# First pair loaded by heads, key penalties in two halves, a rest on GpSimd, twelve units reordered

## The chip, the cores and the metric

One core of one Trainium2 chip runs the whole program in one launch. The metric is the device time of one execution in microseconds (us). A profiled execution has its own time, and a span, from the first to the last instruction that the profile shows. A difference of under about 0.5% (3.5 us) is what a measurement of this kernel cannot tell from no change.

## What is computed

The reference is clustered attention followed by two MLPs. Shapes: batch 2, 8 heads, 768 tokens, head size 64, 16 clusters.

```
c_n = centroids / norm;  q_assign = argmax(q_n . c_n);  k_assign = argmax(k_n . c_n)
mask = q_assign[..., :, None] == k_assign[..., None, :]
scores = where(mask, q k^T / 8, -1e9);  attn = softmax(scores);  x = attn v
h = max(x w1, x w2, x w3);  x = h w_out            # 1536 x 512 -> 768 -> 512
h = x w_in;  g = max(0.01 h, h);  out = g w_out2   # 512 -> 2048 -> 512
```

## The kernel before, in words

Two heads make a pair, and there are 8 pairs. A pair has 6 units: one head (j) and 256 queries (g) each. A unit holds two score blocks i of 128 queries by 768 keys. Products are as precise as float32: an operand is split into a rounded part and a rest, and both go through fp32r matmuls. The cluster mask is inside the scores: 16 more contraction rows hold the one-hot cluster of a query (tile q2, rows 64 to 79) and, for a key, 0 or -2^100 (tile k2, the same rows). These are the key penalties.

The program is written in short operations whose order is fixed by hand. The string `BEGIN` gives the order of the first twelve units and of everything for pairs 1 to 3 that runs beside them; `ORDER` gives the repeating order after that, and it is not touched. An operation goes to one engine, and each engine runs its own in the order in which the string has them, waiting where an operand is not there. So an operation that waits holds everything behind it on that engine. The DMAs of all steps are issued by SyncE (SP), in the same order, one after the other.

Names in the string: `S i:n` scores of block i of unit n (PE, L659; `SA` and `SB` are its two halves, unit 0 alone), `M` the row maximum (DVE, L665), `X` the exponentials (ACT, L671), `R` the inverse of the row sums (DVE, L679, L680), `Q` the normalisation (POOL, L685), `T k:n` transposes (PE, L692), `E` their way out of PSUM (ACT L705 or DVE L707), `V` the product with the values (PE, L716), `Y` its store. For pair p: `LD@p` loads q and k, `QH KH QL KL` round them and take the rests (L419 to L430), `Dq Dk Dl Dm Da Db` copy them to the operand tiles by DMA (L598), `G C H Na Nb W FA FB O P` find the clusters and make the one-hot rows.

Pair 0 has a way of its own, since nothing can hide it. `Z`, a head (a, b) and a letter make its operands without DMAs: q and r round the queries into q1 and q2, k and j the keys into the two halves of k1 (ACT, L419), l and m are the rests of queries (L427) and keys (L430). `Gq` and `Gk` are the products of queries and keys with the centroids (PE, L465), both heads in one; `Na Nb W FA FB` with q or k find the clusters (DVE, L476 to L516); `UQ` and `UK` turn the one-hot of head a (PE, L532), `CQ` and `CK` copy it into q2 and k2 (ACT), `OT`, `PA` and `D2` do the same for head b through a DMA. `Hd` is a one-column copy on POOL which waits for the key one-hot and so holds POOL back until then. `I n` is n idle matmuls on zeros (`nought`): PE work whose result nobody reads, as the two runs of `WARM` are. Unit 0 and 1 are head a, units 2 and 3 head b.

Of the kernel before, what the change touches and what calls it, by code (L numbers as in the profile page):

```python
# [10 lines left out]
BF16 = mybir.dt.bfloat16  # L11
AF = mybir.ActivationFunctionType
ALU = mybir.AluOpType
# [4 lines left out]
P = 128  # L18
B, H, S, D = 2, 8, 768, 64
C = 16  # L20
# [3 lines left out]
G = 256  # L24
# [22 lines left out]
)  # L47

BEGIN = (
    "Zaq Zbr Gq Zar Zal Naq Zbj Gk Nbq Wq FAq FBq Zaj Nak Nbk Zbq I3 UQ Wk Zak FAk CQ I1 G@1 SA0:0 FBk UK  "  # L50
# [14 lines left out]
)  # L65
AFTER = 12

# [8 lines left out]
ENGINE = {  # L76
    "QH": "A", "QH@1": "P", "QH@2": "P", "QL": "D", "QL@1": "P", "KH": "P", "KL": "P", "W": "P"
}
WARM = (7, 2)
PACE = 0.16  # L80
HALF = S // 2
WP = 512
# [6 lines left out]
def clustered_attention_mlps(  # L89
# [16 lines left out]
    nc = tc.nc  # L106
# [120 lines left out]
    def open_hidden():  # L227

        m["w1"] = mlp.enter_context(tc.tile_pool(name="w1", bufs=1))
# [89 lines left out]
    with ExitStack() as att:  # L319
# [25 lines left out]
        gain, base, gain2, base2 = (lines[:, i : i + 1] for i in range(4))  # L345
# [3 lines left out]
        def several(pool, shape, names, dtype=F32):  # L349
            return [pool.tile(shape, dtype, name=x) for x in names]  # L350

        raw_in = [several(raws, [P, S], (f"rq{i}", f"rk{i}")) for i in range(2)]
# [7 lines left out]
        opnd = [  # L360
            [
                tuple(
                    opn.tile([D + C if x[1] == "2" else P, S], F32R, name=f"{x}_{i}_{j}")
                    for x in ("q1", "q2", "k1", "k2")
                )
                for j in range(2)
            ]
            for i in range(2)
# [32 lines left out]
        st = {}  # L401

        def load_pair(p, what):
            s = st.setdefault(p, {})
            for x in what:
                if x == "v":
                    s["rv"] = raw_v[p % 3]
                    src = v[p].rearrange("p (t h d) -> p t h d", t=NQ, h=2)
                else:
                    s["r" + x] = raw_in[p % 2]["qk".index(x)]  # L410
                    src = (qT if x == "q" else kT)[p]
                nc.sync.dma_start(out=s["r" + x], in_=src)
# [11 lines left out]
        def rest(engine, out, x, hi, scale=1.0):  # L424
            hi = hi.bitcast(F32)
            if scale != 1.0:
                nc.vector.scalar_tensor_tensor(out, x, scale, hi, op0=ALU.mult, op1=ALU.subtract)  # L427
            else:
                e = nc.vector if engine == "D" else nc.gpsimd
                e.tensor_tensor(out, x, hi, op=ALU.subtract)  # L430
# [191 lines left out]
        def first_operands(j, what):  # L622
            s = st[0]
            q1, q2, k1, k2 = opnd[0][j]
            rq, rk = (s[x][j * D : (j + 1) * D] for x in ("rq", "rk"))
            if what == "q":
                rounded("A", q1[0:D], rq, SCALE)
            elif what == "r":
                rounded("A", q2[0:D], rq, SCALE)
            elif what == "k":  # L630
                rounded("A", k1[0:D], rk)
            elif what == "j":
                rounded("A", k1[D:P], rk)
            elif what == "l":
                rest("D", q1[D:P], rq, q1[0:D], SCALE)
            else:
                rest("D", k2[0:D], rk, k1[0:D])

        un, done = {}, {}

# [88 lines left out]
        def scrap(key):  # L729
            if key not in scraps:  # L730
                scraps[key] = small_bank()
            return scraps[key]
# [82 lines left out]
        if True:  # L815
# [3 lines left out]
            sq = sm.tile([P, 1], F32, tag="sq", name="sq", bufs=1)  # L819
            half = sm.tile([P, 1], F32, tag="half", name="half", bufs=1)  # L820
            nc.sync.dma_start(out=ct, in_=cent)
            load_pair(0, "qk")
            load_pair(1, "qk")
            load_pair(0, "v")

            nought = sm.tile([P, TB], BF16, tag="nought", name="nought", bufs=1)
            nc.gpsimd.memset(nought, 0.0)
            warm = third[:, 0:TB]

            def idle(n):  # L830
# [2 lines left out]

            idle(WARM[0])
            make_identity(nc, idf)
# [37 lines left out]
            nc.vector.tensor_copy(cb.rearrange("p n c -> p (n c)"), cps)  # L873
            idle(WARM[1])


            def start(op):

                if op[0] == "I":
                    idle(int(op[1:]))  # L880
                elif op[0] == "Z":
                    first_operands("ab".index(op[1]), op[2])
                elif op == "Hd":

                    nc.gpsimd.tensor_copy(hold, oh0[:, D + 2 * C : D + 2 * C + 1])
                elif op == "Ct":
                    end_third()
                elif op == "D2":
                    operands(0, "2")
                elif op == "w":  # L890
                    take_apart()
                elif op in ("Gq", "Gk"):
                    sims(0, "qk".index(op[1]), scrap(op))
                elif op in ("Naq", "Nak"):
                    near_max(0, "qk".index(op[2]), scrap("G" + op[2]))
                elif op in ("Nbq", "Nbk"):
                    near_eq(0, "qk".index(op[2]))
                elif op in ("Wq", "Wk"):
                    weigh(0, nc.vector, "qk".index(op[1]))
                elif op in ("FAq", "FAk"):  # L900
                    first_max(0, "qk".index(op[2]))
                elif op in ("FBq", "FBk"):
                    first_eq(0, "qk".index(op[2]))
                elif op in ("UQ", "UK"):
                    onehot_up(0, "QK".index(op[1]), scrap(op))
                elif op == "CQ":
                    ps = scrap("UQ").bitcast(BF16)[D : D + C, 0:S]
                    nc.scalar.copy(opnd[0][0][1][D : D + C], ps)
                elif op == "CK":
                    ps = scrap("UK").bitcast(BF16)[D : D + C, 0:S]  # L910
                    up = slice(D, D + C)
                    nc.scalar.activation(
                        opnd[0][0][3][up], ps, AF.Identity, scale=gain[up], bias=base[up]
                    )
                elif op == "OT":
                    for h in range(2):
                        onehot_T(0, h, scrap(op)[:, 256 * h : 256 * h + 256])
                elif op == "PA":
                    penalties(0, scrap("OT"))
                elif op == "in":  # L920
                    until_scores.close()
                    open_inputs()
                elif op == "oh":
                    until_transposes.close()
                    open_hidden()
                elif op == "F":
                    fetch_pieces()
                elif op == "ph":
                    until_exps.close()
                    open_products()  # L930
                    st["first"] = hidden(0, 0)
                elif op == "h":
                    next(st["first"])
                elif op[0] == "x":
                    split_x(0, (int(op[1]),))
                else:
                    raise ValueError(op)
# [21 lines left out]
            for n in range(-2 * NG, NU + 2 * NG):  # L959
                c, r = divmod(n, 2 * NG)  # L960
                for item in ORDER[r].split():
                    if "/" in item:
                        op, by = item.split("/")
                        if 0 <= n - int(by) < NU:
                            ordered(op, n - int(by))
                    else:
                        op, by = item.split("+")
# [79 lines left out]
```

## Time and profile before

| what | value |
|---|---|
| three runs | 697.94 us median, 695.87 to 698.45 |
| the profiled execution | 697.01 us, of which the span is 695.2 us |
| granted TensorE clock, mean over the span | 0.994 |
| PE busy | 684.7 us, 98% of the span |
| DVE busy | 489.7 us, 70% |
| ACT busy | 337.2 us, 49% |
| POOL busy | 219.8 us, 32% |

Busy shares are means over stages with different limits. The profile has PE busy for 98% of the whole, and the chain of waits that ends last has PE on 91% of it. In the forty slices of the span (17.4 us each) PE shows 9 tenths or more in all but the first and the last. The granted clock is in fractions of 2.4 GHz, so that 0.5 is 1.2 GHz.

### The profile page before, as it was taken

How to read it: one execution, taken by the hardware profiler on the slowest of the kernel's cores; microseconds unless marked ns; L12 is line 12 of the kernel's file. 1: busy time of each engine (PE TensorE's matmuls, PEld its weight loads, DVE VectorE, ACT ScalarE, POOL GpSimd, SP SyncE). 2: the span in 40 equal slices, each digit the busy share in tenths (PEclk: the TensorE clock that was granted, in tenths of full speed). 3: DMA queues.
4: the chain of work that ended last, by engine and by line, in shares of the span. 5: the costliest groups of instructions: out<-in, count | busy, mean ns of one | idle time of the engine just before them, and what ended most of it. 6: DMA issues, size and time to landing. Idle time of an engine off the chain costs nothing.

```text
span 695.2 us, 10338 instructions
## 1 busy us (share of the span) xinstructions
PE 684.7 (98%) x3708; PEld 551.2 (79%) x3709; DVE 489.7 (70%) x895; ACT 337.2 (49%) x635; POOL 219.8 (32%) x201
## 2 busy tenths in 40 slices
PE   8899999999999999999999999999999999999997
PEld 5677777787777788888888888888888888888886
DVE  6967888888867398788783798787349847982222
ACT  6877777877777354323231344454434324431120
POOL 4756556565545011011111111322322223312220
PEclk8999999999999999999999999999999999999999
DMA  5647879428401166545551354165215522500102
GB/s 156 194 121 235 208 170 237 141 64 202 109 4 59 44 207 204 174 159 157 175 163 51 118 151 154 62 204 189 91 56 186 167 76 91 181 31 1 56 35 91
DMA packets 30082, 89.96 MB, mean 129 GB/s; under 512 B 4784, under 2 KB 5680, under 8 KB 30032
## 3 DMA queue, kind: packets, MB, share of 16 engines
q1 hardware_dynamic: 30032, 89.32, 42.6%
q8 instruction: 29, 0.48, 0.3%
q14 instruction: 21, 0.17, 0.1%
HBM read 68.16 MB, written 3.15 MB: 103 GB/s over the span
## 4 chain that ended last, share of the span: by engine, by line
PE 91%; DVE 3%; ACT 2%; DMA 1%; issue 1%; POOL 1%; SPq 1%; ACTq 0%; POOLq 0%
PE h L246 13%; PE h L247 13%; PE h L248 13%; PE y L246 9%; PE y L247 9%; PE y L248 9%; PE s L659 8%; PE t L692 7%; PE o L716 7%; DVE mx L665 1%; ACT ee L671 1%; PE t L545 1%; ACT et L705 1%; SPq L598 1%; DMA k<-kh 1%
## 5 line engine op out<-in xcount | busy, mean ns | idle before, releaser
L280 POOL TENSOR_TENSOR hl<-a,hh 128x512 fp32r<-128x512 f32 x66 | 92.1, 1395 | 355.4 <-ACT hh L279 355.4
L246 PE MATMUL h<-xh,wh 128*128 128x512 f32 x408 | 159.3, 390 | 0.0
L248 PE MATMUL h<-xh,wl 128*128 128x512 f32 x408 | 158.8, 389 | 0.0
L247 PE MATMUL h<-xl,wh 128*128 128x512 f32 x408 | 158.7, 389 | 0.0
L665 DVE TENSOR_REDUCE mx<-s 128x1 f32<-128x768 f32 x96 | 90.7, 953 | 33.5 <-PE s L659 30.9
L685 POOL TENSOR_SCALAR ee<-ee,rs 128x768 f32<-128x768 f32 x96 | 93.3, 987 | 63.6 <-DVE rs L680 43.4
L246 PE MATMUL y<-hh,wh 128*128 128x512 f32 x264 | 102.7, 389 | 0.0
L247 PE MATMUL y<-hl,wh 128*128 128x512 f32 x264 | 102.7, 389 | 0.0
L248 PE MATMUL y<-hh,wl 128*128 128x512 f32 x264 | 102.7, 389 | 0.0
L279 ACT CAST hh<-a 128x512 fp32r<-128x512 f32 x66 | 41.1, 623 | 125.9 <-DVE a L273 75.1
L671 ACT ACTIVATE ee<-s,mx 128x768 f32<-128x768 f32 x96 | 87.0, 907 | 18.6 <-DVE mx L665 15.4
L659 PE MATMUL s<-k,q 128*128 128x512 f32 (+3 forms) x384 | 92.2, 362 | 2.6 <-ACT ee L671 2.6
L246 PEld LDWEIGHTS h<-xh,wh 128*128 128x128 f32 x408 | 76.6, 188 | 16.6 <-issue 0.8
L248 PEld LDWEIGHTS h<-xh,wl 128*128 128x128 f32 x408 | 76.6, 188 | 15.9
L247 PEld LDWEIGHTS h<-xl,wh 128*128 128x128 f32 x408 | 76.6, 188 | 15.7
L271 ACT COPY a<-h 128x512 f32<-128x512 f32 x66 | 38.6, 585 | 96.1 <-PE h L248 94.6
L692 PE MATMUL t<-idf,ee 128*128 128x128 f32 x576 | 78.2, 274 | 1.3 <-ACT et L705 0.5
L306 DVE TENSOR_TENSOR acc<-y,acc 128x512 f32<-128x512 f32 x72 | 48.6, 685 | 40.5 <-PE y L248 40.5
L275 DVE SCALAR_TENSOR_TENSOR a<-a,h 128x512 f32<-128x512 f32 x48 | 32.8, 684 | 61.8 <-ACT a L271 61.6
L659 PEld LDWEIGHTS s<-k,q 80*128 80x128 f32 (+1 forms) x384 | 58.6, 190 | 20.5 <-ACT ee L671 8.7
L692 PEld LDWEIGHTS t<-idf,ee 128*128 128x128 f32 x576 | 65.7, 140 | 8.4 <-issue 1.7
L705 ACT COPY et<-t 128x512 f32<-128x512 f32 x96 | 55.6, 589 | 25.8 <-PE t L692 25.2
(103 smaller groups left out, 842.1 us busy)
## 6 DMA issues: line engine op xcount, KB each, us to landing
raw<-in_w SPq DMA_DIRECT2D x56, 512.0 KB, 3.9
low<-in_w SPq DMA_DIRECT2D x56, 511.5 KB, 3.5
q<-qh SPq DMA_DIRECT2D x28, 192.0 KB, 5.7
k<-kh SPq DMA_DIRECT2D x28, 192.0 KB, 5.8
rq<-in_qT SPq DMA_DIRECT2D x8, 384.0 KB, 3.4
rk<-in_kT SPq DMA_DIRECT2D x8, 384.0 KB, 4.2
rv<-in_v SPq DMA_DIRECT2D x8, 384.0 KB, 5.5
out_T<-acc SPq DMA_DIRECT2D x12, 256.0 KB, 2.0
```

The lines of the kernel that those rows point to most:

```text
L246: nc.tensor.matmul(ps, ah, bh, start=(k == 0), stop=False)
L247: nc.tensor.matmul(ps, ah, bl, start=False, stop=False)
L248: nc.tensor.matmul(ps, al, bh, start=False, stop=(k == n - 1))
L280: nc.gpsimd.tensor_tensor(hlo[:, f, :], a, hh[:, f, :].bitcast(F32), op=ALU.subtract)
L306: nc.vector.tensor_tensor(a, ps, a, op=ALU.add)
L659: nc.tensor.matmul(ps[:, lo:hi], a[:, c0 : c0 + P], b[:, lo:hi], start=start, stop=not start)
L665: nc.vector.tensor_reduce(mx, un[n]["s", i], axis=AX.X, op=ALU.max, negate=True)
L671: nc.scalar.activation(e, u.pop(("s", i)), AF.Exp, bias=u.pop(("m", i)), scale=1.0, accum_out=u["sum"][:, i, 0:1],)
L685: nc.gpsimd.tensor_scalar(e, e, un[n]["rs"][:, i : i + 1], 1.0, op0=ALU.mult, op1=ALU.mult)
L692: nc.tensor.transpose(ps[:, kk, i * P : (i + 1) * P], u["e"][i][:, (k + kk) * P : (k + kk + 1) * P], idf,)
L705: nc.scalar.copy(out, ps)
L716: nc.tensor.matmul(un[n]["o"][j * D : (j + 1) * D], v[:, t, j, :], done[p, g, j][:, t, :], start=(t == 0), stop=(t == NQ - 1),)
```

## The change

- Queries and keys of pair 0 are loaded by heads: four DMAs of 64 rows (q a, k a, q b, k b) in the place of two of 128.
- `nought` is written by DVE and no more by POOL.
- `CK` is cut in two: ACT writes the key penalties of the first 384 keys, and DVE, in a new operation `CL`, those of the last 384.
- The rest of head b's keys (`Zbm`) goes from DVE to POOL.
- Idle matmuls: 8 and 2 at the start (7 and 2 before), 2 between `Gq` and `Gk` (none before), 3 behind `Gk` as before, none behind `UQ` (1 before) and none before `SB` (3 before). In all 15 for 16.
- The string `BEGIN`, the order of the first twelve units, is written anew.

```diff
-    "Zaq Zbr Gq Zar Zal Naq Zbj Gk Nbq Wq FAq FBq Zaj Nak Nbk Zbq I3 UQ Wk Zak FAk CQ I1 G@1 SA0:0 FBk UK  "
-    "Zam Hd QH@1 C@1 OT Zbl Dq@1 Zbk SA1:0 CK Zbm I3 SB0:0 SB1:0 M0:0 M1:0 PA S0:1 H@1 QL@1 Na@1 X0:0 M0:1  "
...
+    "Zaq Gq Zal I2 Gk Naq Zak Nbq Wq FAq Zbq FBq I3 UQ Zar Nak Zaj Nbk Zbj Wk SA0:0 Zbk FAk FBk Zam CQ Hd QH@1  "
+    "G@1 Zbm UK SA1:0 CL KH@1 C@1 CK Zbl OT SB0:0 SB1:0 H@1 PA M0:0 Zbr D2 X0:0 M0:1 X1:0 S0:1 S1:1 S0:2  "
...
-WARM = (7, 2)
+WARM = (8, 2)
...
-                rest("D", k2[0:D], rk, k1[0:D])
+                rest("DP"[j], k2[0:D], rk, k1[j * D : (j + 1) * D])
...
-            load_pair(0, "qk")
+            st[0] = {"rq": raw_in[0][0], "rk": raw_in[0][1]}
+            for h in range(2):
+                for x, src in (("rq", qT), ("rk", kT)):
+                    rows = slice(h * D, (h + 1) * D)
+                    nc.sync.dma_start(out=st[0][x][rows], in_=src[0, rows])
...
-            nc.gpsimd.memset(nought, 0.0)
+            nc.vector.memset(nought, 0.0)
...
-                elif op == "CK":
-                    ps = scrap("UK").bitcast(BF16)[D : D + C, 0:S]
+                elif op in ("CK", "CL"):
                     up = slice(D, D + C)
-                    nc.scalar.activation(
-                        opnd[0][0][3][up], ps, AF.Identity, scale=gain[up], bias=base[up]
-                    )
+                    cols = slice(0, HALF) if op == "CK" else slice(HALF, S)
+                    ps, out_ = scrap("UK").bitcast(BF16)[up, cols], opnd[0][0][3][up, cols]
+                    if op == "CK":
+                        nc.scalar.activation(
+                            out_, ps, AF.Identity, scale=gain[up], bias=base[up]
+                        )
+                    else:
+                        nc.vector.tensor_scalar(
+                            out_, ps, gain[up], base[up], op0=ALU.mult, op1=ALU.add
+                        )
```

What the new string does on the engines shows at three places. The first is DVE between the key one-hot of pair 0 (L516) and the first row maxima (L665). Before:

```order
L516 TENSOR_TENSOR oh_205<-e_229,m_0_1_260 128x6x32
L430 TENSOR_TENSOR k_0_0_134<-rk_108,k_0_0_133 64x768
L427 SCALAR_TENSOR_TENSOR q_0_1_135<-rq_107,q_0_1_135 64x768
L430 TENSOR_TENSOR k_0_1_138<-rk_108,k_0_1_137 64x768
L665 TENSOR_REDUCE mx_0_308<-s_126 128x1
```

and now:

```order
L516 TENSOR_TENSOR oh_208<-e_231,m_0_1_267 128x6x32
L430 TENSOR_TENSOR k_0_0_134<-rk_108,k_0_0_133 64x768
L922 TENSOR_SCALAR k_0_0_134<-t_129,lines 16x384
L427 SCALAR_TENSOR_TENSOR q_0_1_135<-rq_107,q_0_1_135 64x768
L665 TENSOR_REDUCE mx_0_311<-s_126 128x1
```

The rest of head b's keys (k_0_1_138) has left this row of work, and half of the penalties (L922) has come into it, ahead of the rest of head b's queries.

The second is POOL from the held copy on (hold, L885 before and L889 now). Names: qh, kh, ql, kl are the rounded parts and rests of pair 1, ee with rs is `Q` (two instructions a unit, ee_114 and ee_115 unit 0, up to ee_120 and ee_121 unit 3), e with desc is `W`. Before:

```order
L885 CAST hold<-oh_205 128x1
L422 TENSOR_SCALAR qh_279<-rq_109 128x768
L422 TENSOR_SCALAR rq_109<-rq_109 128x768
L430 TENSOR_TENSOR ql_320<-rq_109,qh_279 128x768
L422 TENSOR_SCALAR kh_340<-rk_110 128x768
L685 TENSOR_SCALAR ee_114<-ee_114,rs_330 128x768
L496 TENSOR_TENSOR e_282<-e_282,desc 128x384
L685 TENSOR_SCALAR ee_115<-ee_115,rs_330 128x768
L430 TENSOR_TENSOR kl_372<-rk_110,kh_340 128x768
```

and now:

```order
L889 CAST hold<-oh_208 128x1
L422 TENSOR_SCALAR qh_273<-rq_109 128x768
L430 TENSOR_TENSOR k_0_1_138<-rk_108,k_0_1_137 64x768
L422 TENSOR_SCALAR kh_289<-rk_110 128x768
L422 TENSOR_SCALAR rq_109<-rq_109 128x768
L430 TENSOR_TENSOR ql_346<-rq_109,qh_273 128x768
L685 TENSOR_SCALAR ee_114<-ee_114,rs_337 128x768
L685 TENSOR_SCALAR ee_115<-ee_115,rs_337 128x768
L430 TENSOR_TENSOR kl_391<-rk_110,kh_289 128x768
L496 TENSOR_TENSOR e_292<-e_292,desc 128x384
```

The rest of head b's keys stands third, kh went ahead of the two steps of ql, and `W` of pair 1 went behind kl. Behind these rows come, before, the `Q` of units 1, 1, 2, 2 and 3, then kh and `W` of pair 2, the last `Q` of unit 3 and qh of pair 2; now the two `Q` of unit 1, qh of pair 2, the two of unit 2, kh of pair 2 and the two of unit 3.

The third is ACT at the start. Before:

```order
L419 ACTIVATE q_0_0_131<-rq_107 64x768
L419 ACTIVATE q_0_1_136<-rq_107 64x768
L419 ACTIVATE q_0_0_132<-rq_107 64x768
L419 ACTIVATE k_0_1_137<-rk_108 64x768
```

and now, with q_0_1_136 put off to the last place before the exponentials:

```order
L419 ACTIVATE q_0_0_131<-rq_107 64x768
L419 ACTIVATE k_0_0_133<-rk_108 64x768
L419 ACTIVATE q_0_1_135<-rq_107 64x768
L419 ACTIVATE q_0_0_132<-rq_107 64x768
```

On SP the two loads of pair 2 (`LD@2`, into the tiles of pair 0) now stand ahead of the twelve copies of pair 1's operands; before, the first four of these copies stood ahead of the loads. On PE the list of products up to `T0:3` (the first transposes of unit 3) is the same set as before, in another order; behind it `S0:6`, the first scores of pair 1, comes before `T2:3` and no more after it.

## Rows read from the trace of the kernel before

**Rows 1.** Three stretches: length, busy us of PE, PEld, DVE, ACT, POOL, then clock.

```profile
20.00:25.00 5.00, 3.98 (x23) 2.77 (x21) 4.93 (x12) 4.40 (x10) 4.41 (x4) 1.00 1.05 284
25.00:30.00 5.00, 4.47 (x37) 3.17 (x36) 4.81 (x9) 3.81 (x9) 5.00 (x7) 1.00 0.57 148
30.00:35.00 5.00, 5.00 (x39) 4.50 (x40) 3.97 (x8) 4.55 (x10) 3.36 (x4) 1.00 0.51 176
```

**Rows 2.** PE in order of time: start, us, engine, line, tiles, shapes, count.

```profile
5.55 1.52 PE L465 MATMUL t<-cb,rq 128*128 128x32 f32 x12
6.91 2.16 PE L465 MATMUL t<-cb,rk 128*128 128x32 f32 x12
...
33.21 1.04 PE L692 MATMUL t<-idf,ee 128*128 128x128 f32 x8
```

**Rows 3.** The chain of waits that ended last: start, us, what.

```profile
5.17 0.43 PE s L832 x2
...
9.07 1.28 PE s L832 x3
...
11.41 1.44 PE t L545 x8
12.85 0.94 PE s L659 x2
13.79 0.64 PE t L532 x6
...
27.34 0.86 DVE mx L665
```

**Rows 4.** Two short stretches, columns as in rows 1: the clock stands behind POOL.

```profile
7.50:8.00 0.50, 0.50 (x5) 0.50 (x5) 0.46 (x2) 0.50 (x1) 0.00 (x0) 0.57 0.91 369
...
14.00:15.00 1.00, 1.00 (x12) 0.75 (x10) 0.68 (x1) 0.82 (x2) 0.92 (x2) 0.80 0.67 147
```

**Rows 5.** POOL, ACT and DVE up to the first row maximum, in order of time.

```profile
0.72 0.53 POOL L827 MEMSET nought<- 128x512 bf16 x1 [0.29 <-POOLq L1037]
...
4.58 2.57 ACT L419 ACTIVATE q<-rq 64x768 fp32r<-64x768 f32 x3 [2.58 <-DMA rq<-in_qT]
...
5.53 0.95 DVE L427 SCALAR_TENSOR_TENSOR q<-rq,q 64x768 fp32r<-64x768 f32 x1
...
12.28 1.62 DVE L427 SCALAR_TENSOR_TENSOR q<-rq,q 64x768 fp32r<-64x768 f32 x1
...
14.47 0.98 ACT L912 ACTIVATE k<-t,lines 16x768 fp32r<-16x768 bf16 x1 [0.18 <-PE t L532]
...
16.49 1.82 DVE L665 TENSOR_REDUCE mx<-s 128x1 f32<-128x768 f32 x2 [1.10 <-PE s L659]
```

**Rows 6.** POOL from the held copy to pair 2's first rounding, in order of time.

```profile
11.45 0.84 POOL L885 CAST hold<-oh 128x1 f32<-128x1 bf16 x1 [7.51 <-DVE oh L516]
12.27 0.83 POOL L422 TENSOR_SCALAR qh<-rq 128x768 fp32r<-128x768 f32 x1
13.19 1.40 POOL L422 TENSOR_SCALAR rq<-rq 128x768 f32<-128x768 f32 x1
14.68 2.42 POOL L430 TENSOR_TENSOR ql<-rq,qh 128x768 fp32r<-128x768 f32 x1
...
21.50 1.00 POOL L496 TENSOR_TENSOR e<-e,desc 128x384 f32<-128x384 f32 x1 [0.39 <-DVE e L572]
...
23.36 1.82 POOL L430 TENSOR_TENSOR kl<-rk,kh 128x768 fp32r<-128x768 f32 x1
25.17 4.73 POOL L685 TENSOR_SCALAR ee<-ee,rs 128x768 f32<-128x768 f32 x5
```

**Rows 7.** ACT writes pair 1's one-hot rows, in order of time.

```profile
28.23 0.67 ACT L583 ACTIVATE oo<-s,lines 128x384 fp32r<-128x384 bf16 x1 [1.06 <-DVE mx L665]
```

**Rows 8.** DMA issues of the first 34 us: KB each, median us to landing.

```profile
q<-oo SPq DMA_DIRECT2D x4, 24.0 KB, 2.8
```

**Rows 9.** Weight loads of PE, 33 to 75 us: us waited in total, times, longest.

```profile
PEld s L659 <- ACT ee L671: 1.4, 3, 0.8
```

27 rows, old and new, of the table BEGIN are left out of this document.

## The prediction

> **What bounds the kernel now.** The busy shares of the whole say PE, and the first view read after them was busy time by stretch. From 30 us on PE has no idle time worth a name (5.00 of 5.00), and I found none above 1 us before 180 us, in a part whose order stays. Before that it has: 1.02 and 0.53 us are missing in the two stretches from 20 to 30 us, while DVE is busy for 9.74 of the 10 us [rows 1]. So the start is a chain of latencies, then DVE holds PE, then PE runs solid. A solid PE neither gains nor loses, so the change is worth what it moves the point where PE becomes solid. I put that point at T0:3, the first transposes of unit 3, because the set of PE work ahead of it is the same in both orders. It starts at 33.21 us [rows 2]. Whatever this start gains, the end gains, unless PE stalls again later.
>
> The second view was the chain of waits in the first 17 us. PE stands on nearly all of it, and much of that is not work: it runs at 1.2 GHz. The granted clock falls to half near 7.6 us and comes back near 14.4 us [rows 4]. What PE had done before it fell were two idle matmuls and the small products with the centroids. Two idle matmuls take 0.43 us before the fall, three take 1.28 us after it [rows 3]: 0.215 against 0.43 each. The products with the keys take 2.16 us, those with the queries, of the same size, 1.52 [rows 2].
>
> **The change part by part.** The start first, on the assumption that the extra idle matmuls keep the clock at 2.4 GHz.
>
> *nought on DVE.* It frees POOL of 0.53 us ahead of the identity matrix [rows 5], on which the centroids' transpose hangs. The gain on the products' start lies between 0 (the centroids' own transfer ends last) and 0.46; I take 0.3, so they start at 5.25 for 5.55.
>
> *Loads by heads.* ACT waits 2.58 us for the queries and starts at 4.58 [rows 5]; with half the bytes it starts earlier, by at most about a microsecond. Seven roundings at 0.84 us stand before CQ, six before. They end between 9.6 and 10.5, beside the DVE work on the clusters, so the price is 0 to 0.3 and I take 0. The query products need both heads, now the third transfer of four: in hand somewhere between 4.58, when all queries were in before, and 6.91, when the keys were in use [rows 2, 5]. I take it hidden by the centroids' chain, which ends at 5.25.
>
> *Two idle matmuls between the products* put 0.43 us [rows 3] on the path. The key products start at 5.25 + 1.36 (6.91 less 5.55) + 0.43 = 7.05, which is 0.14 later than before.
>
> *The clock.* At full clock the rest costs: key products 1.52 (8.6), three idle 0.65 (9.25), the six turns of UQ 0.32 (9.6), SA0:0 0.5 (10.1), the pair-1 products 0.72 (10.8), UK 0.32 and some 0.2 to land (11.35). The halves are taken from the rows at 1.2 GHz: 1.28, 0.64, 0.94, 1.44 [rows 3]. DVE needs five steps of 0.36 to 0.4 behind the key products, to 10.6, so UK does not wait for it. Before, UK ended at 14.43.
>
> *Penalties in two halves.* CK takes 0.98 for 768 columns [rows 5]. A half lies between 0.49 and 0.98 (if the cost were fixed); I take 0.55 on either engine, so they are there at 11.9, where before it was 15.45.
>
> *Rest of head b's keys off DVE.* DVE now has: one-hot to 10.6, rest of head a's keys to 11.55, penalties to 12.1, rest of head b's queries, then the first maximum. That query rest took 0.95 alone and 1.62 with POOL at work beside it [rows 5]; I take 1.62. The first maximum starts at 13.7 for 16.49: 2.8 us earlier.
>
> *POOL.* It takes one more instruction of 64 x 768 on two inputs. The nearest rows are the rests of 128 x 768: 1.82 alone, 2.42 beside a DVE rest [rows 6]. I take 2.42 for it and 1.82 for ql. From 10.6: hold 0.84, qh 0.83, the new rest 2.42, kh 0.83, scaling 1.40, ql 1.82 bring 18.74; two Q at 0.95 20.64; kl 1.82 and W 1.00 bring 23.46; Q of unit 1, 25.36; qh of pair 2, 26.2; Q of unit 2, 28.1; kh of pair 2, 28.9; Q of unit 3, 30.8 [rows 6].
>
> **The Trainium skill** bears on this place: SBUF — State Buffer, section Who interferes with whom, has a DVE instruction with two SBUF inputs and a POOL instruction that reads SBUF exclude each other, the loser waiting for the whole of the other's. The trace has the loser pay 0.6 to 0.67 us. By the rule, if POOL's rest is the loser behind DVE's 0.95, it takes 2.77 and the sum is 0.35 us worse; by the row it stays.
>
> *DVE.* Before, it went from the first maximum at 16.49 to the ninth at 27.34 [rows 3, 5], 10.85 us. The list between is now shorter by one copy out of PSUM (0.68) and one inverse (0.36): 9.8 us, which brings 23.5; but FA of pair 1 stands there and waits for W, at 23.46, so the ninth maximum starts near 24.8 to 25.8. From there two maxima, three copies and an inverse, 4.2 us, lead to 29 to 30 us. POOL comes last, at 30.8.
>
> *SP.* The two loads of pair 2 stand ahead of pair 1's copies and wait for the last rounding on ACT and for POOL's new rest (14.7). The copies of qh therefore start near 16 us for 13.1. S0:6, their first user, is past 30 us; nothing of them is late. What could be late are the one-hot rows: behind FB and O@1, ACT writes them in 0.67 [rows 7], four copies issue in 2.4 us and land 2.8 us after [rows 8], so 5.9 in all from about 25.3: 31.2, as T0:3 ends at 31.25. Hidden, but with nothing to spare.
>
> *The sum.* T0:3 starts at 30.8 for 33.21: 2.4 us. Behind it PE was solid and I count nothing, though its weight loads for scores still wait 1.4 us in all for exponentials between 33 and 75 us, some of it under running matmuls [rows 9], and these waits could go or grow. 697.01 (695.2 of span and 1.81 around it) less 2.4 is 694.6. The median of the runs is 0.93 above the profiled time, and I put half of that on: **695.0 us**.
>
> **The rivals.**
>
> *The clock falls all the same.* For it: the two added idle matmuls are 0.43 us more activity in a stretch still made of small products, and the two runs of idle matmuls later on are gone. Against it: from 20 to 30 us PE is idle for up to a fifth and the clock stays at 1.00 [rows 1]. Then key products end at 9.2, three idle at 10.5, UQ at 11.1, SA0:0 at 12.1, pair-1 products at 13.5, UK at 14.3, the first maximum between 15.9 and 16.5; POOL starts 0.9 later than above and gets to T0:3 at 31.7, DVE at 31 to 32.3. Gain 0.9 to 1.5: 696.4 on the same footing. The Trainium skill, TensorE: Matmul & The Clock Gate, Part 1, says that activity is judged on a schedule of its own that does not start with the kernel; by that one program draws the fall in some runs and not in others, and the three runs do spread by 2.6 us. No run here shows it directly. Chance 0.33.
>
> *The one-hot rows of pair 1 come late*, and the kernel is slower. W went behind kl on POOL, FA and FB behind W, O@1 and the copies behind them, and S0:6 now stands ahead of T2:3. It decides from the point where ACT starts the rows after 28.2, when it did so before [rows 7]. That needs POOL's rests at 2.42 each, the clock at half (W at 25.9), and FB lengthened beside POOL. Then S0:6 starts at 28.9 + 5.9 = 34.8, 1.1 us behind the 33.7 that it would have needed to keep even: 698.1 on the profiled footing, 698.5 on mine. Against it: three delays at once. Chance 0.10.
>
> *More than the start is gained.* qh and kh of pair 2 are made and copied earlier, so the waits of scores up to 75 us go as well, 0 to 1.4 us [rows 9]; with 1.2 of it the time is 693.8. Chance 0.12.
>
> **How the numbers follow.** The forecast, 694.0 to 696.2 by its own unknowns (0.35 for POOL, 0.3 for ACT, 0.5 at S0:6), has 0.45. A range from 693.0 to 698.4 leaves out the far end of the last gain and of the slow case. Faster by over 0.5% means below 694.45: the last rival, and about a third of the forecast, 0.28. Slower by over 0.5% is above 701.4, which only a stall that I don't see gives: 0.03. The rest, 0.69, is within what a measurement tells from no change.
>
> **What would show it.** The granted clock at 1.00 from 8 to 14 us, key products in about 1.5 us, the first maximum near 13.7, POOL without a pause between the held copy and unit 3's Q, and T0:3 near 30.8 with PE solid behind it. Wrong is the clock step if the three idle matmuls take 1.28 us again; the POOL step if T0:3 waits for DVE or ACT; and the whole if PE shows new idle time past 31 us, first of all before S0:6.

## The result, and the profile after

| kernel | runs | median us | lowest to highest | ratio, 95% interval |
|---|---|---|---|---|
| before | 20 | 697.04 | 695.67 to 699.82 | |
| changed | 20 | 700.9 | 697.59 to 705.98 | 1.0058 [1.0038, 1.0077] |

The change makes the kernel slower, by about 4 us. The forecast was 695.0 us with an upper end of 698.4, so it missed the size and the sign. The profiled execution took 702.88 us, 5.87 more than that of before, so it is a slower one than the median; its span is 701.1 us and its mean granted clock 0.990, for 0.994.

Busy time by stretch comes first, with the columns of [rows 1].

```profile
8.50:9.00 0.50, 0.50 (x4) 0.50 (x3) 0.47 (x2) 0.48 (x2) 0.00 (x0) 0.50 1.00 393
20.00:25.00 5.00, 4.87 (x19) 3.85 (x19) 4.41 (x8) 4.19 (x9) 3.31 (x4) 0.69 0.94 263
25.00:30.00 5.00, 4.92 (x38) 3.56 (x36) 4.67 (x10) 3.82 (x9) 4.35 (x5) 0.97 1.03 232
30.00:35.00 5.00, 3.50 (x26) 2.89 (x25) 3.10 (x7) 3.62 (x8) 4.88 (x7) 1.00 0.71 156
60.00:65.00 5.00, 3.88 (x29) 3.38 (x28) 3.00 (x6) 3.58 (x8) 0.27 (x1) 1.00 0.93 193
65.00:70.00 5.00, 4.44 (x26) 3.10 (x26) 3.35 (x6) 2.36 (x5) 4.62 (x4) 0.66 1.04 257
```

Three things are new against before. The clock fell at 8.3 us in spite of the added idle matmuls, and again at 21.9 and at 66.3. From 30 to 35 us PE is busy for 3.50 of 5 us, where it had been solid [rows 1]. And from 60 to 70 us 1.68 us are missing, in a part that the forecast had left at nothing. PE in order of time shows where:

```profile
6.33 1.50 PE L465 MATMUL t<-cb,rq 128*128 128x32 f32 x12 [0.92 <-DVE q L427]
...
8.09 2.46 PE L465 MATMUL t<-cb,rk 128*128 128x32 f32 x12
10.36 1.47 PE L836 MATMUL s<-nought 128*128 128x512 bf16 x3
...
32.85 0.97 PE L659 MATMUL s<-k,q 128*128 128x512 f32 x4 [1.35 <-ACT ee L671]
...
35.81 1.04 PE L692 MATMUL t<-idf,ee 128*128 128x128 f32 x8
...
64.37 0.61 PE L659 MATMUL s<-k,q 80*128 80x512 f32 x2 [1.11 <-DMA k<-kl]
...
65.99 4.50 PE L716 MATMUL o<-et,rv 128*64 128x256 f32 x24 [0.56 <-DMA rv<-in_v]
```

The products with the queries start at 6.33 for 5.55 and those with the keys at 8.09 for 6.91 [rows 2]. The three idle matmuls take 1.47 us: half clock again, as the 1.28 of [rows 3]. T0:3 starts inside the group at 35.81, its first transpose at 36.25, so 3.04 us late. Behind it the other 2.83 us are lost, most of it around 64 to 70 us: scores wait 1.11 for the rest of the keys (`kl`), the product with the values waits 0.56 for `rv`, and then it takes 4.50 us, most of them at half clock, where before and e2 have 2.81.

Three other engines, in order of time. SP:

```profile
1.16 0.57 SPq L826 DMA_DIRECT2D rq<-in_qT  x1
1.77 0.59 SPq L826 DMA_DIRECT2D rk<-in_kT  x1
2.41 0.60 SPq L826 DMA_DIRECT2D rq<-in_qT  x1
...
51.50 0.58 SPq L142 DMA_DIRECT2D raw<-in_w  x1
...
56.21 1.17 SPq L598 DMA_DIRECT2D k<-kl  x2
59.53 3.32 SPq L412 DMA_DIRECT2D rv<-in_v  x2
```

Then DVE (L922, L665) and ACT (L918, L583, L671):

```profile
15.45 0.67 DVE L922 TENSOR_SCALAR k<-t,lines 16x384 fp32r<-16x384 bf16 x1 [1.72 <-PE t L532]
...
16.16 0.66 ACT L918 ACTIVATE k<-t,lines 16x384 fp32r<-16x384 bf16 x1 [0.93 <-DVE k L922]
...
17.53 1.82 DVE L665 TENSOR_REDUCE mx<-s 128x1 f32<-128x768 f32 x2 [0.24 <-PE s L659]
...
31.25 0.67 ACT L583 ACTIVATE oo<-s,lines 128x384 fp32r<-128x384 bf16 x1 [1.77 <-DVE mx L665]
31.82 0.89 ACT L671 ACTIVATE ee<-s,mx 128x768 f32<-128x768 f32 x1
```

Four places are to be seen. A load of 64 rows keeps SP for 0.6 us, a load of 128 rows 0.43. The second head's queries are issued at 2.41 and land 3.8 us after that, near 6.2; before, the whole tile was issued at 1.16 and landed in 3.4, near 4.6. ACT's half of the key penalties waits for DVE's half. `P@1` (L583) waits 1.77 us on ACT for a row maximum, with the exponentials of `X0:4` behind it, and for these the scores at 32.85 on PE wait. And the weights that `F` fetches (`raw`, `low`) are issued from 51.5 us on, ahead of pair 2's `kl` copies and of `rv`; the 3.32 us of the two `rv` issues hold a wait of 2.6 us for `low` between them.

What waits SP had from 48 to 66 us, and how long its transfers took there:

```profile
SPq L412 <- DMA low<-in_w: 2.6, 1, 2.6
...
SPq L412 <- DMA raw<-in_w: 2.1, 1, 2.1
```

```profile
k<-kl SPq DMA_DIRECT2D x2, 192.0 KB, 8.3
```

### The profile page after: what moved, and what is told of

Its sections match the earlier page's. It is cut to its first block, busy times and chain, and to the rows that moved or that the text cites. A ratio compares the mean times of both kernels' runs of the same rounds, so it can differ in the third digit from the quotient of the medians.

```text
span 701.1 us, 10340 instructions
## 1 busy us (share of the span) xinstructions
PE 687.6 (98%) x3708; PEld 554.0 (79%) x3708; DVE 490.1 (70%) x896; ACT 337.2 (48%) x635; POOL 219.7 (31%) x201
## 4 chain that ended last, share of the span: by engine, by line
PE 89%; DMA 2%; ACT 1%; DVE 1%; SPq 0%; issue 0%; ACTq 0%
PE h L246 13%; PE h L247 13%; PE h L248 13%; PE y L246 9%; PE y L247 9%; PE y L248 9%; PE o L716 8%; PE s L659 7%; PE t L692 7%; DMA raw<-in_w 1%; DMA rv<-in_v 1%; DVE xl L237 1%; PE t L545 0%; ACT et L705 0%; SPq L598 0%; ACT ee L671 0%
## 5 line engine op out<-in xcount | busy, mean ns | idle before, releaser
L665 DVE TENSOR_REDUCE mx<-s 128x1 f32<-128x768 f32 x96 | 90.9, 953 | 38.4 <-PE s L659 36.4
L671 ACT ACTIVATE ee<-s,mx 128x768 f32<-128x768 f32 x96 | 86.9, 906 | 17.6 <-DVE mx L665 12.8
```

Of the source, the lines that this page charges most:

```text
L665: nc.vector.tensor_reduce(mx, un[n]["s", i], axis=AX.X, op=ALU.max, negate=True)
L671: nc.scalar.activation(e, u.pop(("s", i)), AF.Exp, bias=u.pop(("m", i)), scale=1.0, accum_out=u["sum"][:, i, 0:1],)
```

## The experiments

The theory behind the experiments (A in the expectations) is that the loss is the sum of waits which single edits put in, each by itself and each to be seen in its place in the trace. Its rival is that these edits are of no account by themselves, and that the clock, or another place behind the start, makes the time. All kernels were timed in five rounds against before on the chip that they ran on (e on one, f on another, g on a third; the changed kernel was timed with the result alone). So what an edit gives back against the changed kernel is a difference of two ratios, and with both intervals it is known to about 1.7 us either way. All ratios but the changed kernel's lie within the 0.5% of the section on the metric, so what is said of them rests on the intervals: two kernels are told apart where they differ by more than both intervals make together, about 1.7 us against the changed kernel and 1.25 between two of the f and g kernels. The table has each kernel's ratio to before, what that ratio is in us (of 697), and from its one profiled execution the first row maximum, the start of T0:3 and the stretches at half granted clock from 7 to 75 us. One execution can lie far from the median: 702.88 for 700.9 in the changed kernel, 697.53 for 699.04 in e3, 700.75 for 699.05 in f4.

| kernel | median us | ratio, 95% interval | us | first maximum | T0:3 | half clock |
|---|---|---|---|---|---|---|
| before | 697.04 | | | 16.49 | 33.21 | 7.6 to 14.4 |
| changed | 700.9 | 1.0058 [1.0038, 1.0077] | +4.0 | 17.53 | 36.25 | 8.3 to 15.1, 21.9 to 25.3, 66.3 to 69.7 |
| e1_old_order | 697.73 | 1.0011 [0.9998, 1.0024] | +0.8 | 17.44 | 34.14 | 7.7 to 14.5 |
| e2_fetch_late | 698.46 | 1.0029 [1.0015, 1.0043] | +2.0 | 17.60 | 35.62 | 8.0 to 14.8 |
| e3_whole_loads | 699.04 | 1.0022 [1.0006, 1.0038] | +1.5 | 14.93 | 33.42 | 17.8 to 21.2 |
| e4_rows_behind_exp | 699.88 | 1.0032 [1.0017, 1.0046] | +2.2 | 14.79 | 33.27 | 16.8 to 23.6 |
| f1_heads_alone | 698.5 | 1.0014 [0.9997, 1.0032] | +1.0 | 15.94 | 32.65 | 9.0 to 12.4 |
| f2_new_start_old_rest | 697.59 | 1.0003 [0.9992, 1.0014] | +0.2 | 14.28 | 33.51 | 16.3 to 23.1 |
| f3_three_mended | 696.02 | 0.998 [0.9967, 0.9993] | -1.4 | 15.06 | 32.46 | 18.2 to 21.6 |
| f4_halves_alone | 699.05 | 1.002 [1.0008, 1.0033] | +1.4 | 17.71 | 36.18 | 24.3 to 27.7 |
| g1_whole_penalties | 695.04 | 0.9974 [0.9958, 0.999] | -1.8 | 13.93 | 31.84 | none |
| g2_rest_on_dve | 696.85 | 0.9996 [0.9984, 1.0009] | -0.3 | 15.92 | 33.76 | 16.2 to 23.0 |
| g3_no_idle_pair | 695.77 | 0.9986 [0.9973, 0.9998] | -1.0 | 14.15 | 31.82 | 16.4 to 19.8 |
| g4_more_idle | 697.19 | 0.9997 [0.9985, 1.0009] | -0.2 | 16.07 | 35.08 | 20.1 to 26.9 |

The granted clock alone does not make the changed kernel's time: six of its runs have the same mean granted clock, 0.995, and took 697.59 to 705.98 us.

**e1_old_order**: every edit of the change but the new order, with the idle matmuls that stand in the order of before.

```diff
-BEGIN = (the order of the changed kernel)
+BEGIN = (the order of before, with CL put in ahead of CK)
```

> All edits of the change but the new order: the string of before, with CL put right ahead of CK and the three runs of idle matmuls of before. Theory A (most of the loss lies in the new order: the weights' fetch ahead of the value loads, one-hot rows ahead of exponentials): under 698.5 us, no wait of the value products for their loads near 60 to 70 us. Theory B (the loss lies in the loads by heads and the other edits of the start): 700 us or more, with the query products starting past 6.2 us as in the changed kernel.

Measured: +0.8 us in the place of +4.0, though the products start as late (6.34) and the clock falls as early as in the changed kernel. So about 3 of the 4 us go with the new order; e2 and e4 look for the places. This kernel has the loads by heads and the halves of the penalties too, and the 1.0 and 1.4 us that f1 and f4 give for them below are 2.4 together for the 0.8 here; the intervals allow that, but the single prices are soft.

**e2_fetch_late**: `F` goes behind both loads of values.

```diff
-... Y:2 ... V:3 Q1:6 F Da@2 ... LV@1 ... M0:11 LV@2 X0:11
+... Y:2 ... V:3 Q1:6 Da@2 ... LV@1 ... M0:11 LV@2 F X0:11
```

> The changed kernel with one word moved: F (the fetch of two weight pieces, four DMAs of 512 KB) goes behind both LV loads. Theory A (the fetch fills the queue ahead of the last rests of pair 2 and the values): the waits for kl and rv near 62 to 66 us and the second fall of the clock there go, 2.5 to 3.4 us less, near 698. Rival (the DMAs are late by themselves): those waits stay at 1 us or more and the time at 700 or more.

Measured: +2.0, so the early fetch cost about 2 us. SP, PE and the transfer in this kernel:

```profile
53.96 1.18 SPq L598 DMA_DIRECT2D k<-kl  x2
55.19 1.07 SPq L412 DMA_DIRECT2D rv<-in_v  x2
56.30 0.43 SPq L142 DMA_DIRECT2D raw<-in_w  x1
```

```profile
63.68 2.81 PE L716 MATMUL o<-et,rv 128*64 128x256 f32 x24
```

```profile
k<-kl SPq DMA_DIRECT2D x2, 192.0 KB, 2.9
```

The two `rv` issues take 1.07 us in the place of 3.32, the `kl` copies land in 2.9 us in the place of 8.3, and both waits on PE are gone. The clock does not fall here either, and the product of 24 takes 2.81 for 4.50; but that is not shown to be the fetch's doing, since e3 and e4 keep the early fetch and have no fall there.

**e3_whole_loads**: the first pair loaded whole again.

```diff
-            for h in range(2):
-                for x, src in (("rq", qT), ("rk", kT)):
-                    rows = slice(h * D, (h + 1) * D)
-                    nc.sync.dma_start(out=st[0][x][rows], in_=src[0, rows])
+            load_pair(0, "qk")
```

> The changed kernel with queries and keys of pair 0 loaded whole, in two DMAs of 128 rows. Theory A (a load of 64 rows moves its bytes at about half the rate of one of 128): the query products start near 5.4 for 6.3 us, the key products 1 us earlier than in the changed kernel, and the time falls by 0.8 to 1.2. Rival (the start is hidden by POOL and ACT anyway): the products start earlier but the time moves by less than 0.4.

Measured: +1.5, so 2.5 us back, about twice what the delay of the products makes. They start at 5.08 and 6.88 us, 1.25 and 1.21 earlier than in the changed kernel. In this execution the rest came with the clock: it stays up until 17.8 us, the idle matmuls take 0.81, and the first maximum comes 2.6 us earlier. The early fetch is still there, and so are its waits, shorter and with the clock up:

```profile
60.97 0.59 PE L659 MATMUL s<-k,q 80*128 80x512 f32 x2 [0.54 <-DMA k<-kl]
...
62.56 2.81 PE L716 MATMUL o<-et,rv 128*64 128x256 f32 x24 [0.57 <-DMA rv<-in_v]
```

**e4_rows_behind_exp**: `P@1` goes behind `X0:4` on ACT.

```diff
-R:3 P@1 Q1:2 X0:4 E2:1
+R:3 Q1:2 X0:4 P@1 E2:1
```

> The changed kernel with P@1 (ACT writes pair 1's one-hot rows, waiting for the maximum of the bank that they share) moved behind the exponentials X0:4. Theory A (P@1 waits on ACT for M1:4 and holds X0:4, and S0:5 behind it): PE's 1.35 us of idle time near 31.5 us shrinks to under 0.4 and the time falls by about 1. Rival (S0:6 then waits for the later rows): the idle time moves to S0:6 and the time stays within 0.5.

Measured: +2.2, so 1.8 us back. ACT in this kernel:

```profile
27.91 0.90 ACT L671 ACTIVATE ee<-s,mx 128x768 f32<-128x768 f32 x1 [0.31 <-DVE mx L665]
...
29.37 0.67 ACT L583 ACTIVATE oo<-s,lines 128x384 fp32r<-128x384 bf16 x1 [0.47 <-DVE mx L665]
```

The exponentials no longer stand behind the one-hot rows, and PE's wait of 1.35 us for them is gone. From the ninth maximum to T0:3 it takes 6.34 us, and 7.43 to 7.44 in the changed kernel, e2 and e3; f3, g2, g3 and g4, which have this edit too, take 6.34 to 6.35. That 1.1 us doesn't hang on when the start ended. The clock of the start fell elsewhere in this execution (16.8), so the columns ahead of T0:3 say nothing of this edit. Moved behind, the rows were not late either: S0:6 doesn't wait. The early fetch is in this kernel, and SP waits 1.1 and 2.2 us for it, but PE does not; it waited 1.52 us for a normalisation on POOL at 51 us instead.

**f1_heads_alone**: before, with the loads by heads alone (the diff of e3 the other way round).

> The kernel before with one edit: the four loads by heads. Theory A (a half load of 64 rows takes as long as a whole one, so both heads together land later): query products start 0.6 to 0.9 later than 5.55 us, key products 0.7 to 1.2 later than 6.91, and the time is 0.5 to 1.0 us above before. Rival (the cover of the other engines takes it): products late, time within 0.3 of before.

Measured: products at 6.35 and 7.68, 0.8 us later each, the first as in the changed kernel. Here the profile names the transfer itself as what PE waits for:

```profile
6.35 1.50 PE L465 MATMUL t<-cb,rq 128*128 128x32 f32 x12 [0.42 <-DMA rq<-in_qT]
```

In time +1.0, with an interval that just takes in no change. The delay is shown; its price in time is not told from zero by this run alone.

**f2_new_start_old_rest**: the changed kernel's operations up to the first maximum, whole loads, and then the order of before.

```diff
-BEGIN = (order of the changed kernel)
+BEGIN = (its part ahead of M0:0, then what is left of before's in before's order)
```

> The changed kernel's operations up to the first row maximum, with whole loads, followed by the order of before for all that is left. Theory A (the loss of the changed kernel lies in the loads and in the order behind the first maximum, and its start is otherwise good): first maximum at 15 us or earlier where the clock does not fall, and 0.5 to 2 us under before. Rival (the rest of head b's keys on POOL and the halves cost as much as the start gains): within 0.5 of before or above it.

Measured: no gain (+0.2). The first maximum comes 2.2 us earlier than in before, and T0:3 0.3 us later. In this execution the clock fell at 16.3, behind the first maximum, for the same 6.8 us as in before: put off and not saved. Whether all twelve runs went so the runs don't show.

**f3_three_mended**: e2, e3 and e4 together, by the three diffs above.

> The changed kernel with the three mendings together: fetch behind the value loads, whole loads, one-hot rows behind X0:4. Theory A (three separate causes, whose shares add up: 2.4, 1.9 and 1.0 us of the medians): 695.5 to 696.5, under before. Rival (they overlap, since each shortens what the others wait for): 697.5 to 698.5.

Measured: -1.4, and so faster than before, with an interval clear of one. By themselves the three gave 2.0, 2.5 and 1.8, each just clear of the 1.7, 6.3 in all; together 5.4, the same within the intervals. The three faults together account for the whole loss, and what is left of the change is a gain; how the loss splits among them is known only roughly.

**f4_halves_alone**: before, with the penalties in two halves.

```diff
-SA1:0 CK Zbm
+SA1:0 CL CK Zbm
```

> The kernel before with one edit: CL, put ahead of CK. Theory A (ACT's half waits for DVE's, as both read one PSUM tile and write one tile, so they run one after the other): CL 0.67 and CK 0.66 end to end, 1.3 for 0.98, and 0.2 to 0.5 us above before. Rival (they run side by side): penalties there 0.3 us earlier, time at or under before.

Measured: +1.4, more than the 0.2 to 0.5 that I had expected. DVE's half, and ACT's:

```profile
15.53 0.68 DVE L918 TENSOR_SCALAR k<-t,lines 16x384 fp32r<-16x384 bf16 x1 [0.27 <-PE t L532]
...
16.24 0.66 ACT L914 ACTIVATE k<-t,lines 16x384 fp32r<-16x384 bf16 x1 [0.26 <-DVE k L918]
```

They run one after the other: 1.37 us from the start of the first to the end of the second, where the whole tile took ACT 0.98 [rows 5]. That is shown. The profile accounts for 0.2 to 0.4 us of loss, no more: from the start of the penalties to the first maximum it is 2.18 us, and 2.02 in before. The first maximum itself is 1.22 us later, but this execution was late ahead of anything that the edit touches:

```profile
8.37 2.75 PE L465 MATMUL t<-cb,rk 128*128 128x32 f32 x12
10.93 1.47 PE L832 MATMUL s<-nought 128*128 128x512 bf16 x3
...
10.00:12.00 2.00, 2.00 (x9) 1.41 (x9) 1.26 (x5) 0.70 (x1) 0.00 (x0) 1.00 0.00 0
```

PE runs at half pace up to about 14 us here, 1.47 us for three idle matmuls, while the granted clock reads 1.00. The column of the table doesn't show this. Every profile begins so (before: seven idle matmuls in 3.08 us from 1.30 on), and all the others are at full pace by 4 to 7 us. So the price in time is larger than what this one profile shows, and that rest stays open.

**g1_whole_penalties**: f3, with `CK` whole on ACT and no `CL`.

```diff
-SA1:0 CL KH@1 C@1 CK Zbl
+SA1:0 KH@1 C@1 CK Zbl
```

> The mended kernel (fetch late, whole loads, one-hot rows behind X0:4) with the key penalties again in one piece on ACT. Theory A (the halves run one behind the other, 1.3 us for 0.98, and cost in every order): 0.3 to 1.2 us under the mended kernel's 696.0. Rival (in this order ACT is late, and DVE's half pays for the wait): 0 to 0.6 us above it.

Measured: -1.8, the lowest ratio of all, faster than both kernels. By the ratios it is 0.4 us under f3 and by medians 1.0, and their intervals overlap, so the runs don't tell the two apart. ACT, DVE and POOL here:

```profile
12.01 0.98 ACT L912 ACTIVATE k<-t,lines 16x768 fp32r<-16x768 bf16 x1
...
12.28 1.62 DVE L427 SCALAR_TENSOR_TENSOR q<-rq,q 64x768 fp32r<-64x768 f32 x1
13.93 1.82 DVE L665 TENSOR_REDUCE mx<-s 128x1 f32<-128x768 f32 x2
...
13.19 2.40 POOL L430 TENSOR_TENSOR k<-rk,k 64x768 fp32r<-64x768 f32 x1
```

and DVE and POOL in f3, where the clock was up over the same stretch:

```profile
12.03 0.68 DVE L918 TENSOR_SCALAR k<-t,lines 16x384 fp32r<-16x384 bf16 x1 [0.56 <-PE t L532]
12.74 2.29 DVE L427 SCALAR_TENSOR_TENSOR q<-rq,q 64x768 fp32r<-64x768 f32 x1
15.06 1.82 DVE L665 TENSOR_REDUCE mx<-s 128x1 f32<-128x768 f32 x2
...
12.41 1.81 POOL L430 TENSOR_TENSOR k<-rk,k 64x768 fp32r<-64x768 f32 x1
```

The penalties start at the same time in both, 12.01 and 12.03. The half on DVE puts the rest of head b's queries off by 0.46 us, right into POOL's rest (from 12.41 to 14.22 in f3), and there it takes 2.29 for 1.62: 1.13 us on the first maximum. That is what these two executions show and no fixed price of the halves: in g3 (below), which has them too, DVE's rest comes 0.17 us ahead of POOL's, and it is POOL's that takes longer.

```profile
12.79 0.95 DVE L427 SCALAR_TENSOR_TENSOR q<-rq,q 64x768 fp32r<-64x768 f32 x1
...
12.96 2.49 POOL L430 TENSOR_TENSOR k<-rk,k 64x768 fp32r<-64x768 f32 x1
```

The first maximum of g3 is at 14.15 and its T0:3 at 31.82, as in g1 (31.84).

**g2_rest_on_dve**: f3, with the rest of head b's keys back on DVE.

```diff
-                rest("DP"[j], k2[0:D], rk, k1[j * D : (j + 1) * D])
+                rest("D", k2[0:D], rk, k1[j * D : (j + 1) * D])
```

> The mended kernel with the rest of head b's keys back on DVE, in the place in the string where it now stands. Theory A (the move to POOL helps, since DVE is busy without a break and POOL waits at the first normalisation): 0.3 to 1.0 us above the mended kernel. Rival (POOL's chain up to the first normalisation is as tight): within 0.3 of it or under.

Measured: -0.3 for f3's -1.4. DVE in this kernel:

```profile
11.00 2.60 DVE L430 TENSOR_TENSOR k<-rk,k 64x768 fp32r<-64x768 f32 x2
13.63 0.67 DVE L918 TENSOR_SCALAR k<-t,lines 16x384 fp32r<-16x384 bf16 x1
```

Both rests stand ahead of DVE's half of the penalties, which starts at 13.63 and in f3 at 12.03; the first maximum is 0.86 us later. By the two values the move to POOL helps by about 1 us; the two intervals overlap, so the runs alone don't settle it.

**g3_no_idle_pair**: f3 without the two idle matmuls between the products.

```diff
-Zal I2 Gk
+Zal Gk
```

> The mended kernel without the two idle matmuls between query and key products. Theory A (they only stand in the way, 0.43 us on the path, and do not keep the clock up): 0.2 to 0.5 us under the mended kernel. Rival (they keep the clock up in some of the runs): above it by 0.3 or more, with more runs whose clock falls before 15 us.

Measured: -1.0, not told apart from f3. In its profile the clock stayed up until 16.4 us without the pair, so the pair isn't needed for that.

**g4_more_idle**: f3 with four idle matmuls for two, and six for three.

```diff
-I2 ... I3
+I4 ... I6
```

> The mended kernel with four idle matmuls for two between the products and six for three behind them. Theory A (the clock falls in the start for want of work on PE): no fall before 15 us in the profile, a smaller spread of the runs, and 0.3 to 1.0 us under the mended kernel. Rival (idle matmuls are as much in the way as they save): 0.3 or more above it.

Measured: -0.2, which is 1.2 us above f3, with intervals that overlap a little. The clock is up from 8 to 16 us and falls at 20.1:

```profile
8.00:16.00 8.00, 7.32 (x60) 5.19 (x59) 6.95 (x12) 6.01 (x8) 4.14 (x4) 1.00 0.03 10
20.00:24.00 4.00, 3.71 (x13) 3.32 (x14) 3.26 (x7) 3.11 (x8) 3.30 (x3) 0.52 1.05 243
```

The more idle work goes with a first maximum 1.0 us later than f3's, and no gain is seen.

## Why the prediction was wrong, step by step

- **nought on DVE.** Small either way, as forecast. DVE scales the centroids from 3.90 to 3.98 us on (e3, f2, f3 and the g kernels), for 4.37 before, so nearly all of the 0.46 of the bound came. What was left of it hung on PE, which the step did not look at: where the two idle matmuls ahead of the products take 0.59 us, as before, the products start at 5.08 (e3) and 5.22 (f3), near the forecast 5.25; where they take 1.06, still at half pace, they start at 5.63 (f2 and the four g kernels), for 5.55 before. In the changed kernel the loads by heads cover it.
- **Loads by heads: failed.** The step said "I take it hidden by the centroids' chain", and the price was 0. The second head's queries were the third transfer of four, with an issue of 0.6 us for each of them, and half the bytes did not land sooner: 3.8 us after its issue, where the whole tile took 3.4. The products start 0.8 us late with them, alone (f1) or not, and whole loads gave 2.5 us back in time (e3). The bound of that step, 4.58 to 6.91, held the value (6.33); taking it hidden at 5.25 was the error. The releaser that the profile of the changed kernel names, DVE at L427, isn't the cause: in g1 the same DVE instruction runs from 5.34 to 6.29 while the products start at 5.63, and f1's profile names the transfer. (The step has seven roundings ahead of `CQ` for six before; the traces have seven in both, which changes nothing in the sum.)
- **The clock: failed as forecast.** The rival "the clock falls all the same", at 0.33, was right about the fall, and was priced as a gain of 0.9 to 1.5 because nothing else was to go wrong. What the whole step missed is that the fall can come later: of the kernels with whole loads and the new start, none has it before 16 us, and all but g1 have it after (16.2 to 20.1). Of the five kernels with loads by heads four have it by 9 us. The 0.92 us of PE idle ahead of the products [the first row of PE above] go with these loads; that the idle time causes the fall wasn't tried, and e4, which has the loads, waits 0.51 us there and fell at 16.8, speaks against so simple a rule. The Trainium skill, TensorE: Matmul & The Clock Gate, Part 1, has activity judged on a schedule that doesn't start with the kernel; the places of the fall agree with that.
- **Penalties in two halves: failed.** "0.55 on either engine" and at the same time: a half costs 0.66 to 0.68, and ACT's starts behind the end of DVE's in every profile that has the halves. So the penalties take 1.37 us for 0.98. What that costs in time is not settled: 1.4 us alone (f4), of which f4's profile shows 0.2 to 0.4; 1.13 us on the first maximum between g1 and f3, 0.2 between g1 and g3, and no difference clear of the intervals between g1 and either.
- **Rest on POOL: right.** 1.81 us for the forecast 2.42 in the changed kernel, 2.40 in g1, and a gain by the values of g2 and f3, of about 1 us with overlapping intervals. What the step left out is that the rest can hold up DVE's beside it (f3, 2.29 us).
- **One-hot rows: the place was right, the wait was not.** The rival looked at their copies and at S0:6, and decided from an ACT start after 28.2. ACT started them at 31.25, and S0:6 did not wait. What waited was the work behind them on the same engine: `X0:4`, and through the score buffer PE, 1.35 us (e4: 1.8 in time, 1.1 in the profile).
- **"Behind it PE was solid and I count nothing": failed.** The step on SP looked at pair 1's copies alone. `F`, four DMAs of about 512 KB each, had been moved ahead of pair 2's `kl` copies and of `rv`, and SP waited 2.1 and 2.6 us for them: 1.67 us of waits on PE in the changed kernel's profile, 1.11 in e3's, none in e4's, and 2.0 us in time (e2). The fall of the clock behind these waits stands in the changed kernel's profile alone.
- **The sum.** The forecast's start is there once its own assumptions are: in g1, with whole loads, whole penalties and the clock up, the first maximum is at 13.93 (forecast 13.7), T0:3 at 31.84 (30.8), its second part held 0.55 us by POOL as the step had it, and the median is 695.04. Up to the first maximum the chain was read rightly; from there to T0:3 it took 17.9 us for the forecast 17.1, so of the 2.4 us forecast at T0:3 1.4 came. That the median meets the 695.0 is in part luck, since by the ratio the gain is 1.8 us and not the 2.9 that 695.0 was under the median on record (697.94). And it doesn't make the forecast right, which was for the kernel with three faults.

## What to carry to other kernels

When an order is rewritten, follow each moved DMA and each moved wait on its own queue to the first thing behind it, to the end of the moved part and not only to the first milestone: here two moves of one word each cost about 2 us, known to some 1.7 either way. A transfer or an instruction cut in two is two issues and perhaps a wait between them; price the pieces from the nearest rows as serial until a row shows them side by side. Idle matmuls that move a fall of the clock need not remove it (g4); compare such edits by runs, not by one profile.

## What the runs showed of the hardware

- An HBM load of 64 rows kept SP for 0.57 to 0.60 us, one of 128 rows with twice the bytes for 0.43 (with 0.58 for one of them in the changed kernel). From issue to landing the two half loads of queries took 3.2 and 3.8 us, the whole one 3.4 in before and 3.1 in e3.
- A 64 x 768 rest on DVE takes 0.95 us alone; beside POOL it took 1.62 when POOL's instruction was one of 0.83 (g1) and 2.29 when it was a rest of 1.81 (f3). DVE's end lies 0.80 to 0.81 us behind POOL's in both (13.10 to 13.90, 14.22 to 15.03), and in g3, where DVE's rest starts first, POOL's takes 2.49 for 1.81: the one that starts later seems to wait for the whole of the other's, and the prediction's row of 0.6 to 0.67 was only one case of it. The rule in the Trainium skill, SBUF — State Buffer, Who interferes with whom, which the prediction set beside that row, agrees.
- The granted clock falls at different places in kernels that are the same up to there: at 8.3, 8.0 and 16.8 us in the changed kernel, e2 and e4. At the start of every profile PE runs at half pace while the granted clock reads 1.00, up to 4 to 7 us (before: 0.44 us for each of seven idle matmuls, where 0.215 is full pace [rows 3]) and in f4 up to about 14.
- Runs of one kernel spread by 2 to 8 us. Before has 105 runs beside the experiments, and their mean granted clock sorts them in part: 0.997 or 0.998 goes with 695.16 to 696.84 us, 0.993 or 0.994 with 696.96 to 698.56. But the 25 runs at 1.00 took 697.70 to 698.89. A long start at half pace that this clock doesn't show, as in f4, would fit; it wasn't shown, since each kernel has one profile.
